# ReLUs and K copies on VectorE, and a last output in two column parts, in a fused attention and MLP kernel

## The chip, the cores and the metric

The kernel runs on one core of one Trainium2 chip. A core has a matrix engine (TensorE, PE in the profile, with its weight loads as PEld), VectorE (DVE), ScalarE (ACT), GpSimd (POOL), a queue engine that here only starts transfers (SyncE, SP), and 16 DMA engines. The metric is the time of one execution on the device, in microseconds (us). Less is better.

## What is computed

The inputs are q, k and v of shape (4, 8, 768, 64), that is batch, heads, positions and head size, a gain of 512 values, and two weights, 512 x 2048 and 2048 x 512. All are float32. The first half is an attention in which each query attends to 6 chunks of 32 positions at most. They are chosen by an upper bound on the scores, from the least and greatest key of each chunk. The second half is a layer norm with an MLP of two matrix products and a residual.

```
k_min, k_max = min and max of k over each chunk of 32
ub     = sum(maximum(q * k_min, q * k_max), -1)        # causal chunks only
sel    = the 6 chunks of greatest ub, for every query
scores = q @ k.T / 8, where sel and causal, else -1e9
x      = softmax(scores) @ v                           # then (4, 768, 512)
xn     = (x - mean) / sqrt(var + 1e-6) * g_ln
out    = x + maximum(xn @ w_ch1, 0) @ w_ch2
```

## The kernel before

*Tiles.* Positions lie in tiles of 128, six for a batch. A pair of heads is a group g, so there are 16 groups, four for a batch b. A batch is halved again: r = 0 stands for its first three tiles, r = 1 for its last three. Products are in fp16 with sums in fp32 PSUM; transposes of q and k and the bounds of the first groups are in fp32.

*The attention of a group.* `load_qk` and `load_v` fetch from HBM. `turn` transposes q and k on TensorE. `q_copy` and `k_copy` take the transposes out of PSUM as fp16 into the buffers QA and QB, KA and KB, one for each head. For the four groups of the first batch (g < HP, with HP = 4) `k_copy` consists of two ScalarE copies, KA (L275) and KB (L276), for each half i. For later groups it is one copy and two transfers. `k_bound` and `k_diag` make the chunk bounds, `bounds` multiplies them with q, `select` finds the chosen chunks, and `mask_t` and `mask_ring` put the mask into the other rows of QA and QB, so that the mask comes into the scores with the same product. `scores` (L411) multiplies, and ScalarE's exponential (L417) writes pt. `diag` (GpSimd, L424) cuts the causal triangle, `values` (L437) multiplies with v, and `normalise` divides on VectorE.

*The MLP of a half.* `pair_stats`, `stats`, `centre` and `rstd` give the layer norm. `x_t` transposes the centred rows (L497) and multiplies in the gain. `mlp1` makes 256 of the 2048 hidden columns in one piece (m = 0, 2, ... 14): eight products of 384 columns (L512) into the PSUM tile `mm`, then one ReLU on ScalarE that empties it as fp16 (L516). `mlp2` makes 128 rows of the result (tile i) from 16 products of 512 columns (L524, kt = 0 to 15), four to a piece j. They add up in the PSUM tile `yp`, one bank. After the last one VectorE multiplies with 1/std, adds x (L530), and SyncE sends the 128 x 512 tile out (L535).

*Buffers.* `mm` has two slots, each two banks. The scores and `mlp1` share them, so each of their pieces waits until the one two places before it is emptied. All other PSUM tiles share the tag "one" with four slots of a bank each. The weights come by four GpSimd transfers each (`w1_load`, `w2_load`), a quarter of w1's columns, or four values of kt of w2. A one-element copy ahead of each, which reads a result of `k_bound`, keeps it from starting too early.

*What sets the order.* Each piece gets a position: a base from its stage, plus an amount from the table MOVED under its function and its longest matching arguments, else under the empty key (). Pieces are issued in the order of the positions. Those of the list `begin` (the attention of the first batch, its loads and the weights' loads) are "kept": their instructions stand in exactly this order on TensorE, VectorE, ScalarE and GpSimd. For all others the position is a priority: a scheduler that models durations takes the ready instruction of the best position on each engine. Each engine then works in the order so fixed, and stands when its next instruction has to wait. GpSimd's transfers go through one queue, SyncE's through another.

*The first batch is special.* While its second half of attention runs, `mlp1` and then `mlp2` of (b, r) = (0, 0) stand between its pieces. All weights have to arrive in this time.

## Time and profile before

| | us |
|---|---|
| three runs, median (lowest to highest) | 303.6 (302.7 to 303.85) |
| the profiled run, time | 303.4 |
| the profiled run, span from first to last instruction | 301.4 |
| TensorE busy | 288.2 |
| VectorE busy | 190.8 |
| ScalarE busy | 183.5 |
| GpSimd busy | 91.1 |

TensorE's granted clock was 0.997 of full speed over the span. The core read 27.27 MB from HBM and wrote 6.29 MB.

The profile is of one execution. Its page gives the busy time of each engine, then the span in 40 slices of about 7.5 us (each digit is a busy share in tenths), the chain of work that ended last, and groups of instructions: line, engine, operation, out<-in, sizes, count, then busy us, mean ns of one, idle us of the engine just before them and what ended it. Windows give the busy time of each engine in chosen stretches. The timeline gives start and length of each instruction, in us, with the idle time before it and its releaser in brackets. Matmuls are pipelined, so their listed lengths overlap; the distance between starts tells how fast they are issued.

### The profile page before, as it was taken

How to read it: one execution, taken by the hardware profiler on the slowest of the kernel's cores; microseconds unless marked ns; L12 is line 12 of the kernel's file. 1: busy time of each engine (PE TensorE's matmuls, PEld its weight loads, DVE VectorE, ACT ScalarE, POOL GpSimd, SP SyncE). 2: the span in 40 equal slices, each digit the busy share in tenths (PEclk: the TensorE clock that was granted, in tenths of full speed). 3: DMA queues.
4: the chain of work that ended last, by engine and by line, in shares of the span. 5: the costliest groups of instructions: out<-in, count | busy, mean ns of one | idle time of the engine just before them, and what ended most of it. 6: DMA issues, size and time to landing. Idle time of an engine off the chain costs nothing.

```text
span 301.4 us, 7194 instructions
## 1 busy us (share of the span) xinstructions
PE 288.2 (96%) x2753; PEld 195.4 (65%) x2753; DVE 190.8 (63%) x654; ACT 183.5 (61%) x274; POOL 91.1 (30%) x162
## 2 busy tenths in 40 slices
PE   7887998999999999999999999999999999999993
PEld 3874766765777676777767667766666555555541
DVE  7888655679998788999577768577262282011011
ACT  3983997664788667778665674848368524423310
POOL 9559383152444412733230411223021120000000
PEclk9999999999999999999999999999999999999998
DMA  7999999999659649679572210113010110010111
GB/s 131 208 210 198 180 199 196 164 193 204 149 135 187 124 72 165 110 143 148 88 132 62 78 46 2 41 49 90 35 37 0 37 37 35 35 37 35 70 37 71
DMA packets 90226, 31.41 MB, mean 104 GB/s; under 512 B 78416, under 2 KB 87120, under 8 KB 90192
## 3 DMA queue, kind: packets, MB, share of 16 engines
q1 hardware_dynamic: 60416, 23.61, 33.8%
q0 software_dynamic: 29248, 7.34, 24.8%
q8 instruction: 22, 0.36, 0.5%
q14 instruction: 12, 0.10, 0.1%
q10 hardware_dynamic: 528, 0.00, 0.1%
HBM read 27.27 MB, written 6.29 MB: 111 GB/s over the span
## 4 chain that ended last, share of the span: by engine, by line
PE 75%; DMA 8%; POOL 7%; issue 4%; DVE 4%; ACT 1%; POOLq 0%; ACTq 0%
PE yp L524 24%; PE mm L512 24%; PE mm L411 10%; PE sm L437 6%; PE tr L223 4%; DMA w2b<-in_moe_w_ch_dram 4%; DMA w1b<-in_moe_w_ch_dram 4%; PE ub L326 3%; POOL va L214 2%; PE trh L497 1%; POOL pt L424 1%; PE trh L354 1%; DVE xc L482 1%; ACT pt L417 1%; POOL rstd L491 1%
## 5 line engine op out<-in xcount | busy, mean ns | idle before, releaser
L417 ACT ACTIVATE pt<-mm 128x1024 f16<-128x1024 f32 (+1 forms) x96 | 86.2, 918 | 25.7 <-PE mm L411 25.3
L524 PE MATMUL yp<-w2b,hT 128*128 128x512 f16 x384 | 95.9, 379 | 1.5 <-DMA w2b<-in_moe_w_ch_dram 1.5
L512 PE MATMUL mm<-xT,w1b 128*128 128x384 f16 x512 | 94.3, 326 | 0.0
L516 ACT ACTIVATE hT<-mm 128x768 f16<-128x768 f32 x64 | 51.9, 813 | 49.1 <-PE mm L512 48.8
L512 PEld LDWEIGHTS <-w1b 128*128 128x128 f16 x512 | 48.9, 98 | 29.9 <-issue 0.2
L524 PEld LDWEIGHTS <-hT 128*128 128x128 f16 x384 | 36.4, 98 | 31.8
L424 POOL TENSOR_SCALAR_AFFINE_SELECT pt<-pt 128x768 f16<-128x768 f16 x32 | 28.8, 899 | 89.1 <-ACT pt L417 89.1
L530 DVE SCALAR_TENSOR_TENSOR ot<-yp,rstd,x 128x512 f32<-128x512 f32 x24 | 17.9, 746 | 45.9 <-PE yp L524 45.9
L411 PE MATMUL mm<-QA,KA 128*128 128x128 f16 (+2 forms) x224 | 34.5, 245 | 1.0 <-ACT hT L516 0.5
L411 PE MATMUL mm<-QB,KB 128*128 128x128 f16 (+2 forms) x224 | 34.2, 246 | 0.0
L437 PEld LDWEIGHTS <-pt 128*128 128x128 f16 x672 | 24.6, 98 | 5.6 <-POOL pt L424 1.8
L437 PE MATMUL sm<-va,pt 128*128 128x65 f16 x672 | 26.5, 193 | 1.4 <-POOL pt L424 1.3
L411 PEld LDWEIGHTS <-KA 128*128 128x128 f16 x224 | 17.9, 99 | 8.1 <-issue 2.3
L471 DVE BATCH_NORM_STATS2 bst<-x 128x6 f32<-128x128 f32 x96 | 21.9, 282 | 0.8
L268 DVE TENSOR_REDUCE kc<-tr 128x12 f32<-128x384 f32 x32 | 17.6, 549 | 6.6 <-PE tr L223 4.9
L411 PEld LDWEIGHTS <-KB 128*128 128x128 f16 x224 | 18.0, 98 | 3.5 <-issue 0.8
L446 DVE RECIPROCAL rden<-sm 128x6 f32<-128x6 f32 x32 | 6.1, 191 | 19.7 <-PE sm L437 19.6
L447 DVE TENSOR_TENSOR x<-sm,rden 128x384 f32<-128x384 f32 x32 | 17.8, 557 | 1.0
L223 PE MATMUL tr<-ident_f,qn 128*128 128x128 f32 x96 | 16.2, 278 | 1.3 <-DMA qn<-in_q_dram 1.3
L269 DVE TENSOR_REDUCE kc<-tr 128x12 f32<-128x384 f32 x32 | 17.5, 547 | 0.0
L279 ACT CAST kh<-tr 128x384 f16<-128x384 f32 x24 | 11.6, 484 | 9.2 <-DMA KB<-kh 3.2
L223 PE MATMUL tr<-ident_f,kn 128*128 128x128 f32 x96 | 16.2, 278 | 0.0
(87 smaller groups left out, 354.2 us busy)
## 6 DMA issues: line engine op xcount, KB each, us to landing
kn<-in_k_dram SPq DMA_DIRECT2D x64, 96.0 KB, 3.3
qn<-in_q_dram SPq DMA_DIRECT2D x64, 96.0 KB, 3.7
out_dram<-ot SPq DMA_DIRECT2D x24, 256.0 KB, 2.1
va<-in_v_dram POOLq DMA_DIRECT2D x12, 192.0 KB, 5.5
w1b<-in_moe_w_ch_dram POOLq DMA_DIRECT2D x4, 512.0 KB, 7.7
w2b<-in_moe_w_ch_dram POOLq DMA_DIRECT2D x4, 512.0 KB, 11.2
KA<-kh SPq DMA_DIRECT2D x24, 48.0 KB, 2.1
KB<-kh SPq DMA_DIRECT2D x24, 48.0 KB, 2.0
```

Source lines behind the costliest of these rows:

```text
L223: nc.tensor.transpose(pst[:, t * P:(t + 1) * P], src[:, t], ident_f)
L268: nc.vector.tensor_reduce(kc[:, 0, n], view, axis=AX.X, op=ALU.min)
L411: nc.tensor.matmul(sc[:, hh, o:o + w * P], ks[:, t * P:(t + 1) * P], qs[:, s * P:(s + w) * P], start=True, stop=True,)
L417: nc.scalar.activation(pt[:, n0:n1].rearrange("p n h x -> p h n x"), sc[:, :, 0:o].rearrange("p h (n x) -> p h n x", x=P), ACTF.Exp, scale ...
L424: nc.gpsimd.affine_select(out=dv, in_=dv, compare_op=ALU.is_ge, fill=0.0, base=0, pattern=[[0, 2 * TR], [1, P]], channel_multiplier=-1,)
L437: nc.tensor.matmul(pv[:, hh, s2, :], pt[:, where[t, s], hh, :], va[:, hh, t, 0:D + 1], start=(t == 0), stop=(t == s),)
L447: nc.vector.tensor_tensor(xh(b, r)[:, :, 2 * hp:2 * hp + 2, :].rearrange("p s h d -> p h s d"), pv[:, :, :, 0:D], rden.to_broadcast([P, 2, ...
L471: nc.vector.bn_stats(h["st"][:, i, hp], xh(b, r)[:, i, 2 * hp:2 * hp + 2].rearrange("p h d -> p (h d)"),)
L512: nc.tensor.matmul(hp_[:, i, 0:TR * P], w1b[:, kt, (m + i) * P:(m + i + 1) * P], h["xT"][:, kt], start=(kt == 0), stop=(kt == KT1 - 1),)
L516: nc.scalar.activation(h["hT"][:, m:m + 2], hp_[:, :, 0:TR * P], ACTF.Relu, scale=HS)
L524: nc.tensor.matmul(yp, h["hT"][:, kt, i * P:(i + 1) * P], w2b[:, kt, :], start=(kt == 0), stop=(kt == KT2 - 1),)
L530: nc.vector.scalar_tensor_tensor(ot, yp, h["rstd"][:, i:i + 1], xh(b, r)[:, i].rearrange("p h d -> p (h d)"), op0=ALU.mult, op1=ALU.add,)
```

## The change

Four of the eight ReLUs of the first `mlp1`, (b, r) = (0, 0), are done by VectorE (m = 2, 6, 10 and 14) as a maximum with 0 and a product. For the four groups of the first batch, the KB copy of the second half (i = 1) is done by VectorE. The last tile of the output (b = 3, r = 1, i = 2) is made in two column parts: 16 products for columns 0 to 383 (pieces j = 0 and 1), which are then scaled, added and sent; then 16 products for columns 384 to 511 (j = 2 and 3) in the same `yp` tile, likewise. The table MOVED has new amounts for most functions; the rows shown are a few of them.

```diff
@@ k_copy
             nc.scalar.copy(KA[g % NK][0:64, c], pst[0:64, :])
-            nc.scalar.copy(KB[g % NK][64:P, c], pst[64:P, :])
+            (nc.scalar.copy if i == 0 else nc.vector.tensor_copy)(KB[g % NK][64:P, c], pst[64:P, :])
             return
@@ mlp1
-        nc.scalar.activation(h["hT"][:, m:m + 2], hp_[:, :, 0:TR * P], ACTF.Relu, scale=HS)
+        if (b, r) == (0, 0) and m % 4 == 2:
+            nc.vector.tensor_scalar(
+                h["hT"][:, m:m + 2], hp_[:, :, 0:TR * P], 0.0, HS, op0=ALU.max, op1=ALU.mult,
+            )
+        else:
+            nc.scalar.activation(h["hT"][:, m:m + 2], hp_[:, :, 0:TR * P], ACTF.Relu, scale=HS)
@@ mlp2
-        for kt in range(4 * j, 4 * j + 4):
+
+        n, cs = 4, slice(0, DM)
+        if (b, r, i) == (B - 1, NR - 1, TR - 1):
+            n, cs = 8, slice(0, DM - P) if j < 2 else slice(DM - P, DM)
+        for kt in range(n * j % KT2, n * j % KT2 + n):
             nc.tensor.matmul(
-                yp, h["hT"][:, kt, i * P:(i + 1) * P], w2b[:, kt, :],
+                yp[:, cs], h["hT"][:, kt, i * P:(i + 1) * P], w2b[:, kt, cs],
                 start=(kt == 0), stop=(kt == KT2 - 1),
             )
-        if j == 3:
+        if kt == KT2 - 1:
             ot = outp.tile([P, DM], F32, name="ot", tag="ot")
             nc.vector.scalar_tensor_tensor(
-                ot, yp, h["rstd"][:, i:i + 1], xh(b, r)[:, i].rearrange("p h d -> p (h d)"),
+                ot[:, cs], yp[:, cs], h["rstd"][:, i:i + 1], xh(b, r)[:, i].rearrange("p h d -> p (h d)")[:, cs],
                 op0=ALU.mult, op1=ALU.add,
             )
             s = TR * r + i
-            nc.sync.dma_start(out[b, s * P:(s + 1) * P, :], ot)
+            nc.sync.dma_start(out[b, s * P:(s + 1) * P, cs], ot[:, cs])
@@ MOVED
...
         "load_v": {
-            (2,): -0.087, (3, 0): -0.13, (3, 1): -0.568, (4,): -0.551, (5,): -0.547, (6,): -0.163,
...
+            (): -0.126, (0, 0): -0.129, (0, 1): -0.083, (2,): -0.087, (3, 0): -0.13, (3, 1): -0.568,
+            (4,): -0.551, (5,): -0.582, (6,): -0.163, (7,): 0.215, (8,): -0.124, (9,): 0.35,
...
         "mlp1": {
-            (0, 0, 2): -0.016, (0, 0, 6): 0.106, (0, 0, 10): 0.098, (0, 0, 14): 0.069,
...
+            (): -0.294, (0,): -0.023, (0, 0): 0, (0, 0, 2): -0.016, (0, 0, 6): 0.106,
+            (0, 0, 8): 0.034, (0, 0, 10): 0.132, (0, 0, 12): 0.034, (0, 0, 14): 0.103,
...
         "mlp2": {
-            (): -0.156, (0, 0, 1, 0): -0.071, (0, 0, 1, 3): 0, (0, 0, 2, 0): -0.051, (0, 1): -0.154,
...
+            (): -0.177, (0, 0, 1, 0): -0.092, (0, 0, 2, 0): -0.072, (0, 0, 2, 1): -0.179,
...
+        "w2_load": {
+            (0,): 0.265, (1,): 0.256, (2,): 0.189, (3,): 0.183,
+        },
...
```

By these amounts `load_v(4)` now stands between the second and the third `w2_load` in the kept order (before, it stood after the fourth), the q transposes of `turn(0, "qn", 1)` stand ahead of `x_t(0, 0, 0)` (before, just after it), and several pieces of the later batches change places.

## The prediction

> **What bounds the kernel now.** First the head of the page (busy time) and its slices of 7.5 us: TensorE is the bound, ScalarE and DMA are full only early.

> ```profile
> PE 288.2 (96%) x2753; PEld 195.4 (65%) x2753; DVE 190.8 (63%) x654; ACT 183.5 (61%) x274; POOL 91.1 (30%) x162
> ...
> DVE  7888655679998788999577768577262282011011
> ACT  3983997664788667778665674848368524423310
> ...
> DMA  7999999999659649679572210113010110010111
> ```

> PE's 96% needs care: a matmul of 512 columns is listed with 379 ns, but the chain of waits has 40 of them in 8.65 us, 216 ns each. From 80 us on, starts in the timeline follow at that pace; I count about 2 us of holes up to 297 us. So only holes before that can be won: about 7.5 us up to 30 us, 1.3 us from 30 to 50, 1.7 us at 51, 1.2 us from 70 to 80. Next, therefore, the busy time by stretch:

> ```profile
> 29.00:39.00 10.00, 9.98 (x77) 7.54 (x75) 6.69 (x29) 9.82 (x22) 4.92 (x9) 1.00 1.45 182
> 39.00:51.00 12.00, 11.26 (x116) 8.52 (x114) 7.55 (x24) 11.88 (x19) 7.48 (x14) 1.00 1.27 199
> 51.00:54.00 3.00, 1.46 (x13) 0.94 (x12) 0.67 (x3) 0.35 (x2) 0.25 (x1) 1.00 1.25 192
> 54.00:62.00 8.00, 8.00 (x90) 6.02 (x88) 5.86 (x19) 5.85 (x8) 2.76 (x6) 1.00 1.71 168
> ```

> After the length stand PE, PEld, DVE, ACT, POOL. ScalarE (fourth) is busy 21.7 of 22 us from 29 to 51; DVE (third) 14.2. Then, from 51 to 54, PE does half and all others nearly nothing. PE's timeline shows both kinds of hole:

> ```profile
> 38.20 1.46 PE L512 MATMUL mm<-xT,w1b 128*128 128x384 f16 x8
> 40.21 0.38 PE L411 MATMUL mm<-QA,KA 128*128 128x128 f16 x4 [0.55 <-ACT hT L516]
> ...
> 49.53 1.89 PE L524 MATMUL yp<-w2b,hT 128*128 128x512 f16 x8
> 52.96 0.38 PE L524 MATMUL yp<-w2b,hT 128*128 128x512 f16 x1 [1.54 <-DMA w2b<-in_moe_w_ch_dram]
> ```

> Eight matmuls at 162 ns end issuing at 39.50; PE stands 0.71 us for a ReLU, and 0.26 us twice soon after. At 51.26 it meets the matmul of kt = 8, whose third of w2b is not there: 1.70 us, with everything behind it in PE's order held. The chain names the transfer, and gives the end:

> ```profile
> 40.66 12.26 DMA w2b<-in_moe_w_ch_dram
> ...
> 288.20 8.65 PE yp L524 x40
> ...
> 296.88 0.75 DVE ot L530
> ```

> [...]256 KB of output landed in 2.0 us, 48 KB (L280) in 2.1.

> **The change part by part**, against the profiled span of 301.4 us (its run took 303.4; the three others 302.7 to 303.85, median 303.6, so I add 2.2).

> *ReLUs and K copies.* First ScalarE's groups from 29 to 51.3 us (busy us, mean ns of one, idle before), then DVE's nearest, reads of fp32 PSUM in two sizes, over the whole span:

> ```profile
> L516 ACT ACTIVATE hT<-mm 128x768 f16<-128x768 f32 x7 | 5.6, 812 | 0.1
> ...
> L276 ACT CAST KB<-tr 64x384 f16<-64x384 f32 x4 | 1.9, 474 | 0.0
> ```

> ```profile
> L247 DVE SCALAR_TENSOR_TENSOR q<-tr,q 128x384 f16<-128x384 f32 x12 | 6.6, 548 | 3.6 <-ACT q L246 3.6
> ...
> L247 DVE SCALAR_TENSOR_TENSOR q<-tr,q 128x256 f16<-128x256 f32 x12 | 5.0, 417 | 3.3 <-ACT q L246 3.1
> ```

> In ScalarE's timeline a ReLU takes 0.70 us from start to next start, a copy 0.50. Three of the four moved ReLUs (m = 2, 6, 10, at 33.2, 39.3, 45.3) and all four KB copies (31.3 to 47.2) lie in the full stretch: 3 x 0.70 + 4 x 0.50 = 4.1 us of 22 leave ScalarE; m = 14, at 55.6, is outside. On DVE, 131 ns for 128 columns more gives 548 + 3 x 131 = 0.94 us for 768 columns, and about 0.53 us for a copy: 2.8 + 2.1 = 4.9 us onto 14.2, so 19.1 of 22 us. It fits, but DVE also makes the masks that PE waits for, and its operations behind a ReLU wait while that waits for PE. Bounds of the PE time won: 0 (DVE takes over as the last waiter) to 1.23 us (0.71 + 0.26 + 0.26). I take 1.0: neighbours in the two-slot ring of mm are then freed by two engines in turn.

> *The stall at 51 us.* Two effects. With ScalarE ahead, the scores, the last L512 pair, transposes and bounds that stand behind the stall can come before kt = 8: from 53.17 to 57.40 PE does 4.2 us of just such work without a hole, then 0.9 us of values and 0.4 of scores. Against it, the new table puts load_v(4) ahead of the third w2_load in POOL's fixed order (position -1.697 + 0.189 = -1.508, after -1.542). That queue's loads land in order: w2b's fourth part at 41.9 + 14.3 = 56.2, then va of group 4 at 42.7 + 17.4 = 60.1 and of group 5 at 62.6. A va thus takes 2.5 to 3.8 us of the queue, and the third part would land at 55.4 to 56.7, the fourth at 58.7 to 60.0 (kt = 12 started at 59.78, so hardly late). POOL's extra instructions ahead of it, 0.17 + 1.04 us, are hidden in that. If PE comes 1.0 us earlier and does the 4.2 + 0.9 + 0.4 us first, it reaches kt = 8 at 51.3 - 1.0 + 5.5 = 55.8: 0 to 0.9 us of waiting in place of 1.7. Gain 0.8 to 1.7; I take 1.0.

> *Transposes at 26 us.* The q transposes of group 0 now precede x_t. PE waits there for centred rows (starts at 26.40, 26.92, 27.31, each 56 ns long: holes of 0.47 and 0.33), and three transposes are 3 x 109 = 0.33 us. Gain 0 to 0.3; I take 0.3.

> *The last rows.* Before: 16 x 216 ns + 163 (379 - 216) + 746 = 4.36 us from the group's start to the end of L530. After: 16 x 162 + 164 = 2.76 us to the start of the first read; 384 columns, 746 - 131 = 0.62; a hop of about 0.06 (centring ended at 27.25, its transpose started at 27.31); 16 x 56 (the row of 128-column transposes) + 163 = 1.06; and 128 columns, 746 - 3 x 131 = 0.35. Sum 4.85, so 0.5 us lost[...] and nothing is left to fill PE. Without that wait it would be 2.59 + 1.06 + 0.35 = 4.0, a gain of 0.36. The last transfer is a quarter as large; 48 KB and 256 KB land alike, so I save 0.1 (0 to 0.3); the additional DMA of the first columns is issued 1.4 us earlier on SP and is hidden. Sum +0.4, bounds -0.7 to +0.5.

> *The rest of the tables.* Pieces that are not kept in order (q_ring(11), load_qk(8) and (9), the late mlp1 and x_t) are moved by up to 50 places. With about 2 us of holes after 80 us, SP idle between its loads, and PE always holding another matmul, I count 0, bounds -0.7 and +1.0 for a new wait.

> Sum: -1.0 - 1.0 - 0.3 + 0.4 = -1.9; 303.6 - 1.9 = 301.7.

> **Rivals.**
> *The gain is eaten by the transfer* (no change). PE arrives earlier and waits longer, since w2b's third part is later too: -1.0 + 1.0 - 0.3 + 0.4, some 303.5 to 304. For it: DMA is at nine tenths up to 75 us. Against: the 5.5 us of other work is there.
> *kt = 8 keeps its place* (slower). It decides when it is issued before the scores and the L512 pair behind it: mlp2's default goes from -0.156 to -0.177, which even pulls it forward. Then PE starts it at 55.4 to 56.7 rather than 52.96: +2.5 to +3.8, with -0.3 and +0.4, 306.2 to 307.5, and from 305.1 on if a part of that work comes first. Against: the ReLUs now free mm sooner, so more work is ready first.
> *The change doesn't do what it says*: DVE, in order behind a ReLU that waits for PE, delays mask_ring and selection by the 0.94 us that ScalarE saves; ACT's full stretch ends as PE's did. About 303.3.

> **How the numbers follow.** Half a per cent, 1.5 us, is about what a measurement here can tell from no change. Forecast 0.50 (faster); transfer 0.20 and DVE 0.08 (same, 0.28); kt = 8 in place 0.22 (slower). The forecast's own range is 300.0 to 302.8: its bounds add up to -4.6 and +0.6, but they won't all fall on one side. With the rivals the range is 300.0 to 306.0, which leaves out some two thirds of the slow case (0.14) and the forecast's lowest end (0.05).

> **What would show it.** ScalarE from 29 to 51 down to some 17 to 18 us, DVE up to 19; no PE hole by L516 at 39 us; kt = 8 issued after the last L512 pair and waiting under 1 us; w2b's third landing at 55 to 57; at the end a hole of some 0.7 us in PE between two L524 runs. A wait for w2b of 3 us or more, or DVE late with masks, makes the prediction wrong.

## The result, and the profile after

The changed kernel takes 307.9 us, the median of 4 runs (307.5 to 309.2). The kernel before takes 303.55 us in the runs beside it (302.7 to 303.85). The ratio is 1.016, with a 95% interval of 1.012 to 1.019. So the change makes the kernel slower by some 4.3 us. The prediction was 301.7 us, with a range up to 306.0: wrong in its sign, and outside its range. Two runs of kernels further below, of 306.75 and 306.49 us, are over 1.5% above the fastest of their kernel and are left out of the ratios.

The profiled execution of the changed kernel has a span of 305.6 us (its run took 307.5). Before it was 301.4. First, from the page, the busy times and the slices of TensorE's clock:

```profile
PE 289.9 (95%) x2769; PEld 197.1 (64%) x2769; DVE 196.8 (64%) x663; ACT 179.1 (59%) x266; POOL 90.6 (30%) x162
...
PEclk9999999799999999999999999999999999999999
```

The busy totals moved as the edit says: ScalarE lost 4.4 us and VectorE gained 6.0. Neither is what counts. What is new is the 7 in the row of TensorE's clock, in the eighth slice, from 53 to 61 us. Then the same four stretches as before (after the length stand PE, PEld, DVE, ACT and POOL, then the granted clock):

```profile
29.00:39.00 10.00, 10.00 (x79) 8.00 (x79) 8.08 (x23) 7.66 (x17) 7.14 (x13) 1.00 1.42 180
39.00:51.00 12.00, 11.23 (x113) 8.23 (x112) 9.72 (x36) 9.91 (x15) 5.33 (x9) 1.00 1.36 186
51.00:54.00 3.00, 0.15 (x1) 0.00 (x0) 0.49 (x2) 0.03 (x1) 0.05 (x1) 1.00 1.22 194
54.00:62.00 8.00, 7.34 (x69) 5.52 (x69) 4.21 (x8) 2.65 (x4) 0.30 (x2) 0.79 1.56 172
```

From 29 to 51 us ScalarE went from 21.7 to 17.6 us and VectorE from 14.2 to 17.8, nearly as forecast. PE's busy time there is the same as before. From 51 to 54 PE now does nothing, and after it the clock is 0.79. PE's timeline gives the reasons:

```profile
39.68 0.39 PE L411 MATMUL mm<-QB,KB 128*128 128x128 f16 x4
40.52 0.38 PE L411 MATMUL mm<-QA,KA 128*128 128x256 f16 x2 [0.45 <-ACT hT L521]
...
49.26 1.89 PE L533 MATMUL yp<-w2b,hT 128*128 128x512 f16 x8
54.66 0.38 PE L533 MATMUL yp<-w2b,hT 128*128 128x512 f16 x1 [3.51 <-DMA w2b<-in_moe_w_ch_dram]
54.87 0.33 PE L354 MATMUL trh<-ident_h,MN 128*128 128x128 f16 x3
55.03 0.50 PE L223 MATMUL tr<-ident_f,qn 128*128 128x128 f32 x3
...
55.81 2.67 PE L512 MATMUL mm<-xT,w1b 128*128 128x384 f16 x8
```

The matmul of kt = 8 still follows directly on the first eight, and the transposes and the L512 pieces still follow on it. PE comes to it 0.27 us earlier than before (49.26 against 49.53) and starts it 1.70 us later (54.66 against 52.96). Its hole has grown from 1.70 to 3.67 us. (A hole here is the time from one start to the next, less the usual distance for that shape.) Then eight L512 matmuls last 2.67 us instead of 1.46. Windows that begin and end where the granted clock changes show why (the clock is the third number from the end):

```profile
52.49:55.90 3.41, 1.25 (x12) 0.98 (x12) 0.65 (x2) 0.33 (x1) 0.00 (x0) 1.00 1.24 193
55.90:59.31 3.41, 3.41 (x15) 2.11 (x14) 2.39 (x5) 1.13 (x2) 0.00 (x0) 0.50 1.55 161
59.31:62.73 3.42, 3.42 (x56) 2.99 (x55) 1.85 (x5) 1.29 (x2) 0.94 (x4) 1.00 1.72 195
```

For 3.41 us the clock is at half, which makes 1.7 us of PE's work lost. PE is listed as 100% busy in it. The chain of waits and GpSimd's timeline then show why w2b is late:

```profile
38.77 15.84 DMA w2b<-in_moe_w_ch_dram
```

```profile
36.47 0.75 POOL L166 DMA_DIRECT2D w2b<-in_moe_w_ch_dram  x1 [2.04 <-DMA w1b<-in_moe_w_ch_dram]
37.28 1.02 POOL L204 DMA_DIRECT2D va<-in_v_dram  x1
38.30 0.18 POOL L165 CAST w2b<-kc 1x1 f16<-1x1 f32 x1
38.77 0.76 POOL L166 DMA_DIRECT2D w2b<-in_moe_w_ch_dram  x1 [0.30 <-POOL w2b L165]
```

The third part of w2b is issued 1.9 us earlier than before (38.77 against 40.66) and lands 1.7 us later (54.61 against 52.92), because va of group 4 is now ahead of it. Last, the end, on VectorE and PE:

```profile
300.50 0.62 DVE L539 SCALAR_TENSOR_TENSOR ot<-yp,rstd,x 128x384 f32<-128x384 f32 x1 [1.85 <-PE yp L533]
301.17 1.05 PE L533 MATMUL yp<-w2b,hT 128*128 128x128 f16 x16 [0.71 <-DVE ot L539]
302.26 0.35 DVE L539 SCALAR_TENSOR_TENSOR ot<-yp,rstd,x 128x128 f32<-128x128 f32 x1 [1.15 <-PE yp L533]
```

PE waits for the read of the first columns, a hole of 0.87 us. From the first matmul of the last tile to the end of the span it is still 7.89 us, against 8.16 before.

A first sum from the two traces: +1.97 (stall), +1.7 (half clock), +1.2 (holes from 60 to 290 us: 4.74 against 3.58 us), +0.1 (holes from 30 to 50 us: 1.39 against 1.26), -0.3 (holes up to 30 us: 7.09 against 7.40), -0.3 (end): 4.4, where the spans differ by 4.2.

### The profile page after: what moved, and what is told of

It reads as the page before. It is cut to its first block, busy times and chain, and to the rows that moved or that the text cites. A ratio compares the mean times of both kernels' runs of the same rounds, so it can differ in the third digit from the quotient of the medians.

```text
span 305.6 us, 7242 instructions
## 1 busy us (share of the span) xinstructions
PE 289.9 (95%) x2769; PEld 197.1 (64%) x2769; DVE 196.8 (64%) x663; ACT 179.1 (59%) x266; POOL 90.6 (30%) x162
## 4 chain that ended last, share of the span: by engine, by line
PE 68%; DVE 12%; DMA 10%; ACT 4%; issue 2%; SPq 2%; POOL 1%; ACTq 0%; DVEq 0%; POOLq 0%
PE yp L533 25%; PE mm L512 20%; PE mm L411 8%; PE sm L437 5%; DMA w2b<-in_moe_w_ch_dram 5%; PE tr L223 4%; DMA w1b<-in_moe_w_ch_dram 3%; PE ub L326 3%; ACT pt L417 2%; SPq L195 2%; PE trh L497 1%; DMA qn<-in_q_dram 1%; DVE bst L471 1%; DVE r L255 1%; DVE kc L268 1%
## 5 line engine op out<-in xcount | busy, mean ns | idle before, releaser
L417 ACT ACTIVATE pt<-mm 128x1024 f16<-128x1024 f32 (+2 forms) x96 | 86.2, 921 | 23.6 <-PE mm L411 23.4
L533 PE MATMUL yp<-w2b,hT 128*128 128x512 f16 (+2 forms) x400 | 95.8, 370 | 4.2 <-DMA w2b<-in_moe_w_ch_dram 3.5
L512 PE MATMUL mm<-xT,w1b 128*128 128x384 f16 x512 | 95.0, 329 | 0.4 <-ACT pt L417 0.3
L521 ACT ACTIVATE hT<-mm 128x768 f16<-128x768 f32 x60 | 48.8, 813 | 53.5 <-PE mm L512 50.4
L512 PEld LDWEIGHTS <-w1b 128*128 128x128 f16 x512 | 49.5, 99 | 31.5 <-issue 1.6
L533 PEld LDWEIGHTS <-hT 128*128 128x128 f16 x400 | 37.1, 98 | 31.5 <-issue 0.9
L424 POOL TENSOR_SCALAR_AFFINE_SELECT pt<-pt 128x768 f16<-128x768 f16 x32 | 27.9, 871 | 85.2 <-ACT pt L417 85.1
L539 DVE SCALAR_TENSOR_TENSOR ot<-yp,rstd,x 128x512 f32<-128x512 f32 (+2 forms) x25 | 18.1, 725 | 53.1 <-PE yp L533 51.8
L411 PE MATMUL mm<-QA,KA 128*128 128x128 f16 (+2 forms) x224 | 34.3, 245 | 1.4 <-ACT hT L521 0.8
L411 PE MATMUL mm<-QB,KB 128*128 128x128 f16 (+2 forms) x224 | 34.2, 246 | 0.0
L411 PEld LDWEIGHTS <-KA 128*128 128x128 f16 x224 | 18.4, 100 | 8.1 <-issue 2.1
L268 DVE TENSOR_REDUCE kc<-tr 128x12 f32<-128x384 f32 x32 | 17.6, 550 | 6.7 <-PE tr L223 6.5
L411 PEld LDWEIGHTS <-KB 128*128 128x128 f16 x224 | 17.9, 98 | 3.9 <-issue 1.1
L447 DVE TENSOR_TENSOR x<-sm,rden 128x384 f32<-128x384 f32 x32 | 17.8, 555 | 0.9
L246 ACT ACTIVATE q<-tr 128x384 f16<-128x384 f32 x24 | 11.9, 498 | 10.7 <-PE tr L223 10.5
L501 ACT ACTIVATE xT<-trh,gstr 128x384 f16<-128x384 f16 x16 | 9.2, 580 | 14.0 <-PE trh L497 13.8
L269 DVE TENSOR_REDUCE kc<-tr 128x12 f32<-128x384 f32 x32 | 17.4, 542 | 0.0
L446 DVE RECIPROCAL rden<-sm 128x6 f32<-128x6 f32 x32 | 6.1, 189 | 17.4 <-PE sm L437 17.2
```

The source lines that it names most:

```text
L268: nc.vector.tensor_reduce(kc[:, 0, n], view, axis=AX.X, op=ALU.min)
L411: nc.tensor.matmul(sc[:, hh, o:o + w * P], ks[:, t * P:(t + 1) * P], qs[:, s * P:(s + w) * P], start=True, stop=True,)
L417: nc.scalar.activation(pt[:, n0:n1].rearrange("p n h x -> p h n x"), sc[:, :, 0:o].rearrange("p h (n x) -> p h n x", x=P), ACTF.Exp, scale ...
L424: nc.gpsimd.affine_select(out=dv, in_=dv, compare_op=ALU.is_ge, fill=0.0, base=0, pattern=[[0, 2 * TR], [1, P]], channel_multiplier=-1,)
L447: nc.vector.tensor_tensor(xh(b, r)[:, :, 2 * hp:2 * hp + 2, :].rearrange("p s h d -> p h s d"), pv[:, :, :, 0:D], rden.to_broadcast([P, 2, ...
L512: nc.tensor.matmul(hp_[:, i, 0:TR * P], w1b[:, kt, (m + i) * P:(m + i + 1) * P], h["xT"][:, kt], start=(kt == 0), stop=(kt == KT1 - 1),)
```

## The experiments

Twelve kernels were run in three sets, each beside the kernel before on the same chip. The kernel before had medians of 303.36, 303.10 and 302.94 us in them (38 to 42 runs each, from 302.0 to 306.5).

*Is it the place of va in GpSimd's queue?* Theory: the four w2_load amounts, which put va of group 4 ahead of w2b's third part, are the whole loss. Rival: the order on PE or the other rows also matter much. The amounts were taken out of the changed kernel, and put alone into the kernel before. Up to the stall only GpSimd's order changes in both, and PE has the same instructions in the same order throughout.

```diff
-        "w2_load": {
-            (0,): 0.265, (1,): 0.256, (2,): 0.189, (3,): 0.183,
-        },
```

> The changed kernel without its rows for w2_load: POOL issues all four w2 loads ahead of load_v(4) again, and TensorE's, VectorE's and ScalarE's orders stay those of the changed kernel. Queue theory: the v load between the second and third w2 load makes the stall before kt = 8 (3.5 us of waiting, then 3.4 us at half the TensorE clock). The third part should land 2.5 to 3.8 us earlier than the 54.6 us of the changed kernel, the wait fall to at most 1 us, the clock stay whole, and the time be 307.9 - 3.6 = 304.3 us (303.8 to 304.9). VectorE theory (the moved ReLUs and copies cost it, DVE holds the masks): no change, 307.4 to 308.4.

> The kernel before with only the rows for w2_load: load_v(4) goes ahead of the third w2 load in POOL's order and no other engine's order changes. Queue theory: the third part lands at 55.4 to 56.7 us rather than 52.9, PE waits 4 to 5.5 us at kt = 8, its clock then falls to half for some 3.4 us (1.7 us lost): 303.55 + 2.5 to 3.8 + 1.7 = 307.7 to 309.1 us. VectorE theory: the order of the loads does nothing, 303.0 to 304.1.

Without them the changed kernel takes 302.64 us (18 runs; ratio to the kernel before 0.997, 0.995 to 0.999). With them alone, the kernel before takes 309.63 us (4 runs; 1.018, 1.013 to 1.023). The two timelines of PE, first without and then with them:

```profile
51.59 0.38 PE L533 MATMUL yp<-w2b,hT 128*128 128x512 f16 x1 [0.20 <-DMA w2b<-in_moe_w_ch_dram]
...
52.74 1.46 PE L512 MATMUL mm<-xT,w1b 128*128 128x384 f16 x8
```

```profile
49.54 1.89 PE L524 MATMUL yp<-w2b,hT 128*128 128x512 f16 x8
57.17 0.58 PE L524 MATMUL yp<-w2b,hT 128*128 128x512 f16 x1 [5.74 <-DMA w2b<-in_moe_w_ch_dram]
```

The rows alone cost 5.5 to 5.7 us, by 1.018 and by 1.016 - 0.997 (by the medians 6.3 and 5.2). That is more than the whole loss, so the rest of the change is near zero or a small gain. The first expectation was too high: w2b's third part landed at 51.55, earlier even than in the kernel before (52.92), because the other rows of the new table issue it earlier, at 38.50 against 40.66. The second was a little low: PE waits for w2b, landed at 57.13, through a hole of 5.90 us (listed as 5.74 of idle time), and the clock is at half for 6.8 us:

```profile
51.00:57.00 6.00, 0.43 (x3) 0.10 (x1) 0.24 (x1) 0.24 (x1) 0.26 (x1) 0.86 1.25 193
57.00:62.00 5.00, 4.83 (x20) 2.76 (x20) 2.65 (x7) 1.52 (x2) 0.00 (x0) 0.50 1.59 163
```

(0.14 x 6 / 0.5 = 1.7 us while PE still waits, and 5 while it works.)

*What does the half clock cost by itself?* In the changed kernel, 16 matmuls with a tile of zeros add nothing to yp while PE would wait. (Not shown: the zero tile itself, and lines that keep kt = 8 and the transposes behind it in their places.)

```diff
+            if (b, r, i, kt) == (0, 0, 0, 8):
+                for _ in range(16):
+                    nc.tensor.matmul(yp, zt, w2b[:, 7, :], start=False, stop=False)
```

> The changed kernel with 16 matmuls of 512 columns by a tile of zeros, added to yp between kt = 7 and kt = 8 (3.5 us of TensorE work inside the stall; the sum stays the same). Clock theory: the half clock from 55.9 to 59.3 us comes of the idle stretch before it. With TensorE kept busy the clock stays whole, kt = 8 starts at the same 54.7 us, and 1.7 us come back: 306.2 us (305.8 to 306.7). If the clock falls for another reason, or the half clock hides behind other waits, the time stays at 307.4 to 308.4.

It takes 306.13 us (12 runs; 1.008, 1.006 to 1.010), 1.75 less than the changed kernel. (By the two profiled runs it is 1.52, 305.98 against 307.5. The other three runs of the changed kernel have a mean clock of 0.988 to 0.991, where its profiled one has 0.994, so their clock may have fallen once more.) kt = 8 starts at the same time, 0.5 us later even, since the transfer landed a little later. The clock stays at 1.00:

```profile
51.29 3.62 PE L546 MATMUL yp<-w2b,zt 128*128 128x512 f16 x16
55.13 0.38 PE L547 MATMUL yp<-w2b,hT 128*128 128x512 f16 x1 [0.22 <-DMA w2b<-in_moe_w_ch_dram]
...
56.28 1.46 PE L520 MATMUL mm<-xT,w1b 128*128 128x384 f16 x8
```

So here it was the idle time, not the late data, that brought the clock down: after the hole of 3.67 us it was 0.50 for 3.41 us, and with the 3.62 us of products in that place it stayed at 1.00. That is the 1.7 us of the sum. Less idle time was enough in two other runs: holes of 2.43 and 2.48 us (below) also brought 3.4 us of half clock. The 1.70 us of the kernel before did not.

*Would the order of the prediction have saved it?* The prediction let PE do 5.5 us of other work ahead of kt = 8. The changed kernel and the kernel before are made to do that: kt = 8 to 11 of the first row tile stand behind values(1, 1) on PE. This is an order within one engine, with no wait of its own.

```diff
@@ values
+        if (g, r) == (1, 1):
+            hf["hold"] = nc.cur_bb.bb.instructions[-1].name
@@ mlp2
+        n0 = len(nc.cur_bb.bb.instructions)
...
+        if (b, r, i, j) == (0, 0, 0, 2):
+            for one in nc.cur_bb.bb.instructions[n0:]:
+                if one.engine == nc.tensor.engine:
+                    tc.add_manual_dep(one, hf["hold"], order, reason="order")
```

> The changed kernel with the four matmuls kt = 8 to 11 of the first row tile ordered on TensorE behind values(1, 1). The loads stay as they are, in the late order. Order theory (the transfer hurts only because kt = 8 stands ahead of 5 us of ready work): that work fills the stretch from 51 to 56 us, kt = 8 comes after its landing at 54.6 us, no wait of over 0.5 us, no half clock: 307.9 - 3.7 - 1.7 = 302.5 us (301.8 to 303.6). Rival (that work isn't ready either, being behind VectorE's masks or the transfers of q and k): PE stands at a mask transpose or at a transpose of q instead, and the time is 305.5 to 308.

> The kernel before with only kt = 8 to 11 of the first row tile ordered behind values(1, 1) on TensorE. Order theory: the 1.7 us stall at 51 us is filled with work that is ready, 303.4 - 1.6 = 301.8 us (301.4 to 302.3), unless the fourth part of w2b, at 56.2 us, is then met too early, which costs up to 0.8. Rival (what stands behind is held by the masks and by ScalarE, whose full stretch reaches 51 us here): the hole moves to a mask transpose or to the scores, 303.0 to 303.6.

The changed kernel takes 302.49 us with it (16 runs; 0.996, 0.994 to 0.998), the kernel before 301.59 (5 runs; 0.995, 0.993 to 0.997). In the changed kernel kt = 8 to 11 run at 56.27 without a wait, and only w2b's fourth part is still awaited:

```profile
58.82 0.81 PE L536 MATMUL yp<-w2b,hT 128*128 128x512 f16 x3 [0.65 <-DMA w2b<-in_moe_w_ch_dram]
```

In the kernel before, PE is then busy in all of the stretch that held the stall, and its holes from 50 to 60 us fall from 1.71 to 0.03 us:

```profile
51.00:54.00 3.00, 3.00 (x26) 2.22 (x26) 2.50 (x7) 1.96 (x4) 0.02 (x1) 1.00 1.25 192
```

So the prediction was right that there was enough other work and that va's place then costs little. It was wrong that the change would bring that order. Five runs of the kernel before with the order lie within 0.4 us of each other, where 42 of the kernel before alone spread over 4.4. Probably the stall differs from run to run, and the clock with it: the kernels below that keep the stall show it with 1.7 us and no half clock, or with some 2.5 us, half clock and a mean clock of 0.993 or 0.994. The six slowest of the 121 runs of the kernel before, from 305.9 us on, have this mean clock too; they have no trace.

*The ReLUs and K copies alone.* Only these two edits, in the kernel before.

> The kernel before with only the four ReLUs and four KB copies on VectorE (old table, old loads, old last rows). ScalarE from 29 to 51 us should fall from 21.7 to some 17.5 us busy, VectorE rise from 14.2 to 18. Idle theory (TensorE was not held by ScalarE's total work there, only by one or two ReLUs, and meets the w2 transfer anyway): PE's holes from 30 to 50 us stay at 1.1 to 1.5 us and the wait for w2b's third part grows by what is won: 303.4 us (302.9 to 303.9). Relief theory, as the prediction had it: 1.0 us of holes goes, and 302.4 us (302.1 to 302.7).

302.76 us (14 runs), ratio 0.999, 0.997 to 1.001: no difference, and between the two ranges. The windows show that ScalarE was relieved as in the changed kernel, with PE's busy time hardly above the 9.98 and 11.26 of before:

```profile
29.00:39.00 10.00, 9.99 (x80) 7.66 (x77) 8.35 (x25) 8.05 (x18) 4.70 (x8) 1.00 1.44 182
39.00:51.00 12.00, 11.45 (x117) 8.60 (x116) 9.44 (x35) 9.92 (x15) 8.17 (x15) 1.00 1.28 201
```

PE comes to the MLP's first eight products 0.30 us earlier (49.23 against 49.53). Whether it then spends this at the stall can't be read here: the profiled execution is the slowest of the 14, with 305.6 us. In it w2b landed late, at 53.65, and PE had a hole of 2.48 us, with half clock after it. The two kernels without the stall, compared below, show what is left of it.

*The column parts alone*, in the kernel before: once in one bank, as in the change, and once with the second part in another slot of the tag "one". (In both, the table's amounts for this tile are 0.)

```diff
+            if j == 2:
+                h["yp"] = yp = ps_t.tile([P, DM], F32, name="yp", tag="one")
```

> The kernel before with only the last tile in two column parts (same bank). From the trace of the changed kernel, first matmul of the last tile to the end of the span took 7.84 us against 8.12 before: a gain of 0.3 us, 303.1 us (302.8 to 303.3), because 0.5 us lost to the hole in PE is less than what the quarter-size last transfer and the end after it save. The prediction's sum says a loss of 0.4: 303.8 us.

> As the run with two column parts, but the second part adds up in another yp slot, so another bank. Bank theory (the hole of 0.87 us in PE comes only of the shared bank): no hole, the last L530 starts 0.8 us earlier, 302.3 us (302.0 to 302.6). If PE waits for something else there, or a new bank isn't free: the same as with one bank, 302.8 to 303.3.

In one bank: 303.24 us (22 runs), ratio 1.0005, 0.9985 to 1.0025: no difference, with a hole of 0.88 us in PE at the end. (The 7.84 and 8.12 us of the expectation are 7.89 and 8.16 by the starts in the traces; the gain of 0.3 stays.) (Its profiled execution also had a stall, of 2.43 us, in front of kt = 8.) In two banks: 302.24 us (13 runs), 0.997, 0.995 to 0.999. Its PE runs through, and the last read follows 0.28 us behind the one before it, not 1.15:

```profile
295.56 0.62 DVE L535 SCALAR_TENSOR_TENSOR ot<-yp,rstd,x 128x384 f32<-128x384 f32 x1 [1.85 <-PE yp L529]
296.45 0.35 DVE L535 SCALAR_TENSOR_TENSOR ot<-yp,rstd,x 128x128 f32<-128x128 f32 x1 [0.28 <-PE yp L529]
```

So the wait, a hole of 0.88 us with one yp and none with two, came from sharing yp. The prediction's sum had a wait there too, of 0.62 us for the read and 0.06 for a hop; that there would be one was its author's estimate, which no trace of before showed. The run with two banks gives the second part both a tile and a bank of its own, so it doesn't tell the two apart. Nor does the trace show that the hardware needs the wait: leaving it out in one bank was not tried.

*Put together.* Four kernels: the changed one without the w2_load rows, with the order of kt = 8 to 11 and two banks; the kernel before with the order and two banks; that one with the ReLUs and K copies on VectorE; and the changed one without the w2_load rows and with ReLUs and copies back on ScalarE.

> The changed kernel without the w2_load rows (so that va of group 4 follows w2b's fourth part again), with kt = 8 to 11 of the first row tile behind values(1, 1) on PE, and with the second column part of the last output in a PSUM bank of its own. If the three effects are separate: 302.6 without the rows, minus the 0.36 us hole that stays before kt = 8, minus the 0.87 us hole at the end, so 301.2 to 301.6, and no PE hole of over 0.3 us from 50 to 60 us or after 295 us. If the ReLUs on VectorE are worth anything once the stall is gone, it is up to 1 us below the kernel before with the same two edits; if not, the two agree within 0.5 us.

> The kernel before with kt = 8 to 11 behind values(1, 1) and the last output in two column parts, the second in a PSUM bank of its own; ReLUs and K copies stay on ScalarE, all other rows of the table as before. Adding the measured effects (1.6 for the order, 0.9 for the two banks) to 303.1 to 303.4: 300.6 to 300.9. If the second bank's gain was mostly that a stall happened to be shorter in those runs, 301.2 to 301.6, as the order alone.

> The kernel of the run before plus the four ReLUs and four K copies on VectorE. If these are worth nothing anywhere: equal to it within 0.4 us. If their gain was hidden because PE came earlier to the missing w2b: now that PE has other work there, up to 1.0 us less than it.

> The changed kernel without the w2_load rows and with the ReLUs and K copies back on ScalarE: only the rest of the table and the two column parts of the last output are left. If the ReLUs and copies are worth nothing: 302.2 to 302.9, as without the w2_load rows alone (302.6). If they are worth the 1.0 us that the prediction gave them: about 303.6.

| kernel | us (lowest to highest, runs) | ratio to before (95%) |
|---|---|---|
| changed, no w2_load rows, order, two banks | 301.61 (300.97 to 302.46, 17) | 0.995 (0.993 to 0.997) |
| before, order, two banks | 300.58 (300.49 to 300.88, 6) | 0.990 (0.987 to 0.993) |
| the same with ReLUs and copies on VectorE | 300.39 (300.13 to 301.40, 6) | 0.990 (0.987 to 0.993) |
| changed, no w2_load rows, ReLUs and copies on ScalarE | 302.79 (302.13 to 305.58, 22) | 0.999 (0.997 to 1.001) |

The first two are within 0.02 us of the ranges given for separate effects (301.2 to 301.6 and 300.6 to 300.9): order and banks add up. The second and third differ by 0.19 us, less than can be told apart. They are the fastest of all. The last one lies in its range for "worth nothing" (302.2 to 302.9), and its ratio of 0.999 is not distinct from the 0.997 of the same kernel with them on VectorE.

Why are the ReLUs worth so little? The hole of 0.71 us in the kernel before, at 39.50, ended with the ReLU of m = 6. The last matmul of its product had started at 36.65, and ScalarE came to it only at 39.34. So this hole was ScalarE's backlog:

```profile
39.34 1.51 ACT L516 ACTIVATE hT<-mm 128x768 f16<-128x768 f32 x2
```

In the third kernel VectorE does this ReLU, at 37.03, and the scores that use its slot start at 39.52 without a wait. Here are VectorE, ScalarE and PE of that kernel:

```profile
37.03 0.96 DVE L519 TENSOR_SCALAR hT<-mm 128x768 f16<-128x768 f32 x1
```

```profile
39.72 0.81 ACT L523 ACTIVATE hT<-mm 128x768 f16<-128x768 f32 x1 [1.55 <-PE mm L514]
```

```profile
38.22 1.46 PE L514 MATMUL mm<-xT,w1b 128*128 128x384 f16 x8
39.52 0.39 PE L411 MATMUL mm<-QA,KA 128*128 128x128 f16 x4
39.74 0.39 PE L411 MATMUL mm<-QB,KB 128*128 128x128 f16 x4
40.58 0.38 PE L411 MATMUL mm<-QA,KA 128*128 128x256 f16 x2 [0.45 <-ACT hT L523]
```

The next scores, at 40.58, use the slot of m = 8. ScalarE has been idle for 1.55 us and waits for PE's own product of m = 8. Its ReLU starts as soon as the product is there, at 39.72, and takes 0.81 us. PE has only 0.44 us of scores for the other slot of mm, and then needs this one: a hole of 0.62 us, with no backlog on ScalarE at all. This one is a round trip through a ring of two slots. So the hole of 0.71 us went, but the one behind it grew from 0.26 to 0.62; a third went from 0.26 to 0.15. PE's holes from 30 to 50 us are 0.77 us against 1.30 in the second kernel. Of these 0.53 us, 0.28 is left when PE reaches the MLP's first eight products (49.12 against 49.40), and 0.19, not distinct from none, in the time.

## Why the prediction was wrong, step by step

*The stall at 51 us: this step failed.* It took -1.0 us, with bounds of -0.8 to -1.7. The error is in the words "the scores, the last L512 pair, transposes and bounds that stand behind the stall can come before kt = 8". They did not: kt = 8 kept its place, and PE stood for 3.67 us, not 0 to 0.9. The run with that order forced shows how much hung on it: 302.49 instead of 307.88 us.

The price of the load was right: va took 3.7 us of the queue (2.5 to 3.8 forecast). That w2b's third part landed at 54.61 us, before the 55.4 to 56.7 forecast, was luck: other rows of the new table let the second part land at 47.58 rather than 49.54, and the prediction did not count that. In the kernel before with the w2_load rows alone, without this help, the third part landed at 57.13.

The prediction had the right outcome as a rival, "kt = 8 keeps its place", at 0.22, with 306.2 to 307.5 us. That this is so near the 307.88 measured is in part luck too: kt = 8 starts 1.7 us later, not 2.5 to 3.8, and half clock (1.7) and later holes (1.2), which the rival did not have, made up for it. Against the rival the prediction set that the ReLUs free mm sooner, so that more work is ready first. But kt = 8 follows directly on kt = 7 with the old table and with the new one, with the ReLUs on ScalarE and on VectorE: none of these moves it, and neither did it need the amount for mlp2 that the rival named. The step put a guess on what the scheduler would do in place of the order that the trace of before showed. What holds kt = 8 there in the scheduler is not shown.

*A term that was missing: the clock.* No case of the prediction, the slow rival included, had PE's clock fall behind a long wait. It costs 1.7 us by the trace, and the run with the zero products bears it out (1.75). In the trace of before the hole was 1.70 us and the clock stayed at 1.00, so that trace could not show it.

*ReLUs and K copies, -1.0 forecast: mis-sized.* ScalarE at 17.6 us (17 to 18 forecast), VectorE at 17.8 (19 forecast), 957 and 560 ns for the operations on VectorE (0.94 and 0.53 us forecast) are right or nearly so. The gain on PE's path was 0.3 us at 49 us, and nothing that the time shows: 0.999 in one kernel, 0.19 us between two others. The bound of 1.23 us added up three holes as if each could go by itself, and 1.0 of it was taken. The first, of 0.71 us, was ScalarE's backlog and went. PE then came earlier to the next ReLU, whose product it had only just made, and waited 0.62 us there, in the changed kernel too (39.90 to 40.52).

```profile
L517 DVE TENSOR_SCALAR hT<-mm 128x768 f16<-128x768 f32 x3 | 2.9, 957 | 1.7 <-PE mm L512 1.6
L276 DVE CAST KB<-tr 64x384 f16<-64x384 f32 x4 | 2.2, 560 | 1.4 <-ACT KA L275 1.4
```

(These are VectorE's groups in the changed kernel, from 29 to 51.3 us.)

*Transposes at 26 us, -0.3 forecast: 0.* PE still waits twice for centred rows, and then for their ScalarE copy:

```profile
26.25 0.23 PE L497 MATMUL trh<-ident_h,xc 128*128 128x128 f16 x1
26.64 0.23 PE L497 MATMUL trh<-ident_h,xc 128*128 128x128 f16 x1 [0.16 <-DVE xc L482]
27.03 0.40 PE L497 MATMUL trh<-ident_h,xc 128*128 128x128 f16 x4 [0.17 <-DVE xc L482]
27.93 0.49 PE L497 MATMUL trh<-ident_h,xc 128*128 128x128 f16 x6 [0.50 <-ACT xT L501]
```

The q transposes ahead of them fill 0.23 us in which PE had waited for the first of these rows. The two holes between the rows were 0.47 and 0.33 us and are 0.33 and 0.34. But the q transposes are now missing behind the rows, and there PE waits 0.67 us for ScalarE's copy. Over this stretch its lead on the kernel before grew only from 0.25 us (25.59 against 25.84) to 0.29 (29.41 against 29.70).

*The last rows, +0.4 forecast: about -0.3 in the trace, nothing measurable in time.* The compute part went as worked out: reads of 0.62 and 0.35 us, 16 matmuls in 1.05, a wait between them, 4.91 us from the group's start to the end of the last read against 4.85 forecast. What was undervalued is the transfer at the end, 0.1 us saved in the forecast: 64 KB landed in 1.66 us and 256 KB in 2.03, and the end of the span followed 1.29 against 1.69 us behind. That is 0.8 us.

*The rest of the tables, 0 forecast with bounds of -0.7 and +1.0.* PE's holes from 60 to 290 us were 3.95 to 4.74 us in four kernels with the new table (the changed one, those with only the w2_load rows out or only the order, and the first of the table above), and 3.31 to 3.58 in four with the old (before, and the three with the order): +0.4 to +1.4. That this shift is what separates 301.61 from 300.39 us in the table above is likely, but no run takes single rows away. (The bounds of the five parts of the prediction add up to +0.7 at the upper end, not +0.6; nothing hangs on it.)

## What to carry to other kernels

When a change moves a load within a queue, look at who waits for the load that is pushed back, and take that instruction to stay where it stands in its engine's order, unless something is seen to move it. A wait on the matrix engine has a second price once the clock falls: here none after a hole of 1.70 us, but 1.7 us more after those of 2.43 to 3.67. And when an engine is relieved because others wait for it, ask at each wait whether it is behind, or has just been given the work by the very engine that waits. Holes of the first kind go; behind them, one of the second kind can grow.

## What the runs showed of the hardware

```profile
8.20:11.62 3.42, 2.10 (x19) 1.79 (x19) 2.36 (x11) 2.56 (x7) 3.35 (x8) 1.00 1.70 210
11.62:15.03 3.41, 3.41 (x24) 3.20 (x22) 1.71 (x10) 2.30 (x6) 0.01 (x1) 0.50 1.56 212
```

- One load of v ahead of w2b's third part took 3.7 us of the queue (51.3 - 47.6 from landing to landing), with 192 KB; w2b's 512 KB behind it took 3.3 us (54.6 - 51.3). So in this stretch the bytes alone don't give a load's share of the queue.
